# A decode kernel of two layers: late values a column at a time, the MLP's rows in two banks, and eight places for W2 blocks in place of ten

## The chip, the cores and the metric

One core of one Trainium2 chip runs the program. The metric is the device time of one execution in microseconds; the median of the runs counts. A profile of one execution, taken by the hardware profiler, shows the instructions of TensorE (PE for matmuls, PEld for weight loads), VectorE (DVE), ScalarE (ACT), GpSimd (POOL) and SyncE (SP, which here only asks for loads), the clock granted to TensorE, and the traffic of the core's 16 DMA engines.

## What is computed

One token passes twice through attention with a key and value cache and through an MLP with relu. All of it is float32; the cache of 32 heads with 8192 keys and values each is 268 MB, and both layers read the same cache and the same weights.

```python
def _A_ref(x, k_cache, v_cache, wq, wo):
    B, Sq, D = x.shape                       # 1, 1, 640
    H, Dh = 32, 128
    q = (x @ wq).reshape(B, Sq, H, Dh).transpose(0, 2, 1, 3)
    scores = jnp.einsum("bhqd,bhkd->bhqk", q, k_cache) * (Dh ** -0.5)
    p = _softmax(scores, axis=-1)
    o = jnp.einsum("bhqk,bhkd->bhqd", p, v_cache)
    return o.transpose(0, 2, 1, 3).reshape(B, Sq, H * Dh) @ wo

x = A_x
x = x + _A_ref(_layernorm(x), A_k_cache, A_v_cache, A_wq, A_wo)
x = x + relu(_layernorm(x) @ B_w1) @ B_w2
x = x + _A_ref(_layernorm(x), A_k_cache, A_v_cache, A_wq, A_wo)
x = x + relu(_layernorm(x) @ B_w1) @ B_w2
```

## The kernel before

**Loads and the ring.** Keys, values and most of W2 (12 of its 14 blocks of 128 rows) stream through one tile in SBUF, `ring`, of 4760 units; a unit is 8 float32 columns of 128 partitions, 4 KB. `todo` lists every load in order: heads 0 to 31, W2 in four runs of 4, 4, 2 and 2 blocks, then heads 31 to 0 for the second layer, and W2 again. A head's cache comes in pieces: a key piece is a row of 512 keys for each of four partition groups or a part of it, a value piece a block of 4 columns of 128 or a part of it. `pump` (L205 to 223) asks for the next load on the SP queue as soon as `place` finds room; `release` (L237) frees a piece once it is read and calls `pump`. The list is strictly in order: if the load at its head finds no room, all behind it wait. Eight semaphores serve SP's loads in turn, so a load also waits until the one eight before it has landed.

**Kept pieces.** The second layer goes through the heads backwards, so the pieces that were read last are not freed at the end of the first layer and are not loaded again. `KEPT` = 3960 units are kept: head 31, head 30 from its third unit on, and 160 units of head 29's keys. The other `W2_PLACES` = 800 units (ten blocks) are W2's at the end of the first layer; its last run waits until two blocks are read. The two small units of head 30 that are not kept are loaded beside the ring, into the tiles `wct` and `mix`, as soon as these are read for the last time (`load_beside`, L225).

**A head.** PE multiplies the keys by the query into one bank, VectorE takes maxima, ScalarE the exponentials, VectorE transposes them (`pT`), and PE multiplies the values (`values`, L526): for each of four partition groups one matmul with 4 weight columns and 512 moving columns a block, so that 16 rows come out of which 4 sums are wanted. Of the result (`outs`, 128 x 512) the right rows are summed by PE against `ind` (`summed_rows`, L572) after a copy to SBUF by VectorE and ScalarE (`copied_rows`, L565).

**The tail of a layer** begins with its last head (L819). While its keys and values land, the output projection of the others is finished, and the first part of the MLP, `hidden` (L639), is computed from them: four partition groups of 448, 448, 416 and 416 columns side by side in one bank, `acc`. The last value pieces are a whole block and two halves of one. Behind them: `copied_rows`, one matmul to keep PE busy, `summed_rows` into the column `o`, `hidden` once more with `o` and `mix` (the last head's share through the output projection and W1, combined beforehand), and the last head's output projection into `pd`. VectorE copies 256 columns of `acc` to SBUF and ScalarE the others; three matmuls (L866) turn them into columns, VectorE takes the relu into `hT`, four small matmuls (L879, L887) do the rest columns, and 14 times four matmuls (L454) multiply W2's blocks: 0, 1, 2, 3, the two rest blocks, and 4 to 11. The layer norm's spread (`deviations`, `spread_of_rows`) is computed between W2's blocks, from `pd`, and the result is scaled at the end. In the first layer the next one's layer norm and queries follow; in the last the output goes out.

## Time and profile before

| | us |
|---|---|
| median of 3 runs | 1349.75 (1349.57 to 1350.23) |
| profiled execution, its own time | 1351.18 |
| its span, first to last instruction | 1349.4 |
| PE busy in it | 800.5 (59%) |
| VectorE busy | 250.8 (19%) |
| DMA traffic | 574.52 MB, mean 426 GB/s |

The span is what the trace covers; the execution's own time has some 1.8 us more. Times in the rows are microseconds from the span's start. A DMA share of 1.00 means that all 16 DMA engines are busy; a packet counts in the stretch in which it starts, so the share can pass 1. The time to landing of a load runs from its request to the moment at which all of it is there.

### The profile page before, as it was taken

The numbers are of one execution on the slowest core, as the hardware profiler recorded it, in microseconds if no ns is written. First come the engines' busy times: TensorE is split into PE (matmuls) and PEld (weight loads), VectorE is DVE, ScalarE is ACT, GpSimd is POOL, SyncE is SP. The second block draws the span as 40 slices with busy tenths as digits, with TensorE's granted clock in tenths as the row PEclk, the third lists the DMA queues.
The fourth block names the chain that finished last, engine by engine and source line by source line (L and its number), as shares of the span: only waits on it lengthen the run. The fifth ranks groups of instructions, "written<-read, shape, count | busy, mean of one in ns | idle before, by whom it ended". The sixth has DMA issues, their size and how long they took to land.

```text
span 1349.4 us, 13603 instructions
## 1 busy us (share of the span) xinstructions
PE 800.5 (59%) x6086; PEld 271.4 (20%) x6086; DVE 250.8 (19%) x794; ACT 58.5 (4%) x149; POOL 2.9 (0%) x10
## 2 busy tenths in 40 slices
PE   3455554564755755467588765455466554756777
PEld 1111111121211211122143211112121111211223
DVE  1111121221212111122122211122111121112121
ACT  0000000000000000000000000000000000000000
POOL 0000000000000000000000000000000000000000
PEclk8787677887878787788799767788778788878789
DMA  9999999999999999999999999999999999999997
GB/s 405 436 427 430 439 439 417 446 417 445 429 432 425 444 424 429 443 413 419 427 386 427 433 439 424 431 437 422 438 435 427 423 436 434 432 415 444 419 429 314
DMA packets 22673, 574.52 MB, mean 426 GB/s; under 512 B 2516, under 2 KB 2648, under 8 KB 5464
## 3 DMA queue, kind: packets, MB, share of 16 engines
q1 hardware_dynamic: 19592, 529.84, 91.5%
q10 hardware_dynamic: 3024, 43.83, 7.6%
q8 instruction: 47, 0.77, 0.2%
q14 instruction: 10, 0.08, 0.0%
HBM read 573.65 MB, written 0.00 MB: 425 GB/s over the span
## 4 chain that ended last, share of the span: by engine, by line
DMA 64%; PE 27%; DVE 5%; ACT 1%; issue 1%; another core or an unknown queue 1%; ACTq 0%; SPq 0%; DVEq 0%
DMA ring<-in_kv 64%; PE ps L483 13%; PE outs L532 8%; DVE h_t L494 2%; DVE pt L512 1%; ACT p L508 1%; DVE p L551 1%; PE pm L499 1%; PE px L422 1%; PE acc L454 0%; PE px L454 0%; PE px L629 0%; DVE pT L514 0%; PE pm L561 0%
## 5 line engine op out<-in xcount | busy, mean ns | idle before, releaser
L483 PE MATMUL ps<-ring,spread_q 128*32 128x512 f32 (+3 forms) x2104 | 325.6, 769 | 314.7 <-DMA ring<-in_kv 309.6
L532 PE MATMUL outs<-ring,pT 128*4 128x512 f32 (+1 forms) x2080 | 267.3, 656 | 38.6 <-DMA ring<-in_kv 21.6
L483 PEld LDWEIGHTS ps<-ring,spread_q 128*32 128x32 f32 x2104 | 77.0, 137 | 498.5 <-issue 292.2
L494 DVE TENSOR_REDUCE h_t<-ps 128x1 f32<-128x512 f32 x64 | 44.3, 692 | 614.9 <-PE ps L483 614.9
L508 ACT ACTIVATE p<-ps,h_t 128x512 f32<-128x512 f32 x64 | 44.0, 687 | 1225.5 <-DVE h_t L506 1225.5
L532 PEld LDWEIGHTS outs<-ring,pT 128*4 128x4 f32 x2080 | 52.2, 92 | 194.3 <-issue 167.7
L561 PE MATMUL pm<-ones,p 128*128 128x1 f32 x120 | 23.0, 260 | 94.9 <-DVE p L551 94.9
L547 DVE TENSOR_SCALAR p<-outs,ind 128x128 f32<-128x128 f32 x60 | 21.1, 351 | 256.1 <-PE outs L532 256.1
L551 DVE SCALAR_TENSOR_TENSOR p<-outs,ind,p 128x128 f32<-128x128 f32 x180 | 63.1, 351 | 6.4
L512 DVE STREAM_TRANSPOSE pt<-p 128x512 f32<-128x512 f32 x64 | 46.5, 727 | 58.5 <-ACT p L508 58.5
L499 PE MATMUL pm<-row_of,h_t 128*128 128x16 f32 x128 | 25.7, 276 | 49.9 <-DVE h_t L494 49.0
L561 PEld LDWEIGHTS pm<-ones,p 128*128 128x128 f32 x120 | 17.8, 188 | 151.4 <-DVE p L551 150.1
L499 PEld LDWEIGHTS pm<-row_of,h_t 128*128 128x128 f32 x128 | 19.4, 191 | 110.4 <-DVE h_t L494 108.5
L422 PE MATMUL px<-pair,ln_xc 128*32 128x256 f32 x280 | 34.6, 396 | 4.4 <-ACT mix L637 4.4
L629 PE MATMUL px<-w_t,wct 128*128 128x448 f32 (+1 forms) x80 | 35.1, 553 | 1.1 <-ACT wct L622 1.1
L521 PE MATMUL pm<-ind,h_t 128*128 128x1 f32 x128 | 23.6, 254 | 18.3 <-ACT p L508 18.3
L521 PEld LDWEIGHTS pm<-ind,h_t 128*128 128x128 f32 x128 | 22.2, 202 | 37.2 <-ACT p L508 28.4
L454 PE MATMUL acc<-pair,o_cols 128*32 128x160 f32 x496 | 22.5, 323 | 0.6 <-DVE o_cols L583 0.6
L422 PEld LDWEIGHTS px<-pair,ln_xc 128*32 128x32 f32 x280 | 15.7, 113 | 21.4 <-ACT mix L637 8.5
L562 DVE TENSOR_SCALAR o_cols<-pm,h_t 128x1 f32<-128x1 f32 x60 | 13.1, 219 | 30.3 <-PE pm L561 30.3
L506 DVE TENSOR_REDUCE h_t<-pm 128x1 f32<-128x16 f32 x64 | 11.2, 175 | 32.4 <-PE pm L499 32.4
L454 PEld LDWEIGHTS acc<-pair,o_cols 128*32 128x32 f32 x496 | 15.7, 117 | 4.9 <-issue 2.4
(110 smaller groups left out, 208.4 us busy)
## 6 DMA issues: line engine op xcount, KB each, us to landing
ring<-in_kv SPq DMA_DIRECT2D x24, 4096.0 KB, 32.1
ring<-in_kv SPq DMA_DIRECT2D x11, 6144.0 KB, 35.5
ring<-in_kv SPq DMA_DIRECT2D x31, 2048.0 KB, 30.7
pair<-in_wqo ACTq DMA_DIRECT2D x13, 2560.0 KB, 24.4
ring<-in_kv SPq DMA_DIRECT2D x14, 1024.0 KB, 12.5
ring<-in_w SPq DMA_DIRECT2D x4, 1280.0 KB, 26.7
w_t<-in_w ACTq DMA_DIRECT2D x1, 4320.0 KB, 28.7
pair<-in_wqo ACTq DMA_DIRECT2D x3, 1280.0 KB, 13.0
```

Of the source, the lines that this page charges most:

```text
L422: nc.tensor.matmul(pq[32 * j : 32 * j + 32, :n], xc[:, c : c + 1].to_broadcast([P, 32]), wq_t[g][:, c, j * n : (j + 1) * n], start=(c == 0 ...
L454: nc.tensor.matmul(acc[32 * g : 32 * g + 32, :DR], col.to_broadcast([col.shape[0], 32]), wt[:, g * DR : (g + 1) * DR], start=first, stop=last,
L483: nc.tensor.matmul(hd.ps[32 * g : 32 * g + 32, c : c + n], spread_q[:, 3 - r : 35 - r], tile_of[:, at + g * n : at + (g + 1) * n], start=f ...
L494: nc.vector.tensor_reduce(hd.nm, hd.ps, AX.X, ALU.max, negate=True)
L499: nc.tensor.matmul(pt[:, :16], hd.nm.to_broadcast([P, P]), row_of.rearrange("p g r -> p (g r)"), start=True, stop=True,)
L508: nc.scalar.activation(hd.p, hd.ps, AF.Exp, bias=hd.low, scale=1.0, accum_out=hd.l)
L512: nc.vector.transpose(pt, hd.p)
L521: nc.tensor.matmul(pt[:, :1], hd.l.to_broadcast([P, P]), ind[:, 4:5], start=True, stop=True)
L532: nc.tensor.matmul(hd.out[32 * g : 32 * g + 4, r : r + m].rearrange("p r d -> p (r d)"), hd.pT[:, 4 * i : 4 * i + 4], tile_of[:, v : v + m ...
L551: nc.vector.scalar_tensor_tensor(oc[:, r], hd.out[:, r], ind[:, r : r + 1], oc[:, r - 1], op0=ALU.mult, op1=ALU.add,)
L561: nc.tensor.matmul(pt[:, :1], oc[:, 3], ones, start=True, stop=True)
L629: nc.tensor.matmul(pt[:, :n], wct[:, c], w1_t[:, c, f : f + n], start=(c == 0), stop=(c == NB - 1),)
```

## The change

- Head 29's units are cut anew: three units of keys that are loaded twice, one of 320 units that is kept, and then the four value blocks. 4120 units are kept, and W2 has 640 places (eight blocks) at the end of the first layer.
- In the tail only the first two value blocks are computed as before. The later pieces go through `late_values`: a column of `pT` at a time, spread over 32 weight columns, against 128 moving columns, summed in a bank of their own into one row a group. The row sums of the first two blocks (`sums_of_rows`) are computed behind the first late piece; at the end one copy of 128 columns and one matmul add the late sum.
- `hidden` writes columns 0 to 255 of a group into the bank `acc` and the others into `px`, so that the copy of the first bank need not wait for the second.
- The four small matmuls of the rest columns (`hidden_rest`) and the last head's output projection (`pd`) move between W2's blocks, the former ahead of the third, the latter ahead of the first rest block; the two matmuls that kept PE busy go.
- The loads into `wct` and `mix` are asked for behind W2's fourth block (`MIX_BEHIND`).

```diff
+    ("k", [(0, 0, 512), (1, 0, 128)]),
+    ("k", [(1, 128, 384), (2, 0, 256)]),
+    ("k", [(2, 256, 128)]),
+    ("k", [(2, 384, 128), (3, 0, 512)]),
+] + [("v", [v]) for v in V_ALL]
...
-DROPPED = {29: 9, 30: 2}
-KEPT = 3960
-W2_PLACES = 800
+KEPT_UNITS = {29: [3], 30: [2, 3, 4], 31: range(6)}
+KEPT = 4120
+W2_PLACES = 640
+MIX_BEHIND = 3
...
+    def late_values(hd, late, piece, where, first, last):
+
+        b, r, m = piece
+        tile_of, at = at_of[key(*where)]
+        for k in range(m):
+            for g in range(4):
+                i = 4 * (4 * b + g) + r + k
+                v = at + (g * m + k) * DH
+                nc.tensor.matmul(
+                    late[32 * g : 32 * g + 32],
+                    hd.pT[:, i : i + 1].to_broadcast([P, 32]),
+                    tile_of[:, v : v + DH],
+                    start=first and k == 0,
+                    stop=last and k == m - 1,
+                    skip_group_check=True,
+                )
+        release(*where)
...
     def hidden(ph, col, wt, first, last):
-        for g in range(4):
-            f, n = F_AT[g], F_ROWS[g]
...
+        for half, tile_of in enumerate(ph):
+            for g in range(4):
+                a = H_CUT * half
+                n = F_ROWS[g] - H_CUT if half else H_CUT
...
-        for a, (piece, at) in enumerate(pieces):
-            values(hd, piece, at, a == 0, a == len(pieces) - 1)
-            if a == 1:
+        for a, (piece, at) in enumerate(pieces[:2]):
+            values(hd, piece, at, a == 0, a == 1)
+            if a == 0:
                 next(rest)
-            if a == 2:
-                at_once(rest)
         rows = copied_rows(hd)
-        keep_busy(1, 128)
+        at_once(rest)
+        for a, (piece, at) in enumerate(pieces[2:]):
+            late_values(hd, late, piece, at, a == 0, a == len(pieces) - 3)
+            if a == 0:
+                pt = ps_m.tile([P, 512], F32, name="pm")
+                sums_of_rows(pt, rows, False)
+        o_late = work.tile([P, 2 * DH], F32, name="q_row")[:, :DH]
+        nc.vector.tensor_copy(o_late, late)
+        nc.tensor.matmul(
+            pt[:, :WIDE], o_late, one_of_each.to_broadcast([P, WIDE]), start=False, stop=True
+        )
         o = work.tile([P, 1], F32, name="c_ol")
-        summed_rows(hd, rows, o)
+        nc.vector.tensor_scalar(o, pt[:, :1], hd.rl, 0.0, op0=ALU.mult, op1=ALU.add)
...
-        nc.vector.tensor_copy(hr[:, : 2 * P], ph[:, : 2 * P])
-        nc.scalar.copy(hr[:, 2 * P : F_ROWS[2]], ph[:, 2 * P : F_ROWS[2]])
-        nc.scalar.copy(hr[:64, F_ROWS[2] :], ph[:64, F_ROWS[2] : F_ROWS[0]])
+        for c in range(2):
+            nc.vector.tensor_copy(hr[:, c * P : (c + 1) * P], ph[0][:, c * P : (c + 1) * P])
+        nc.scalar.copy(hr[:, H_CUT : F_ROWS[2]], ph[1][:, : F_ROWS[2] - H_CUT])
+        nc.scalar.copy(hr[:64, F_ROWS[2] :], ph[1][:64, F_ROWS[2] - H_CUT : F_ROWS[0] - H_CUT])
...
             if a == 2:
+                hidden_rest()
+            if a == 4:
+                times_rows(pd, wo_t[last // HG][:, last % HG], o, True, True)
...
+            if a == 7:
                 ss = deviations(x1, s1)
-            if a == 8:
+            if a == 10:
                 r1 = spread_of_rows(ss)
...
-            if L == 0 and a == 1:
+            if L == 0 and a == MIX_BEHIND:
+                load_beside(wct.rearrange("p c d -> p (c d)"), 0, NB * P)
                 load_beside(mix, 0, DFF)
```

PE in the first layer's tail, from the last head's first value block to the second `hidden`. Before (`outs` are the values' sums, `pm` the row sums, `acc<-w_t` and `acc<-mix` the two parts of `hidden`):

```order
L532 MATMUL outs_107<-ring,pT 4x512 x8
L642 MATMUL acc<-w_t,ln_xc 32x448 x2
L642 MATMUL acc<-w_t,ln_xc 32x416 x2
L532 MATMUL outs_107<-ring,pT 4x512 x4
...
L532 MATMUL outs_107<-ring,pT 4x256 x8
L388 MATMUL px<-w_t 128x128
L576 MATMUL pm<-ind,p 128x64 x4
L642 MATMUL acc<-mix,c_ol 32x448 x2
```

After:

```order
L528 MATMUL outs_107<-ring,pT 4x512 x4
L661 MATMUL acc<-w_t,ln_xc 32x256 x4
L661 MATMUL px<-w_t,ln_xc 32x192 x2
...
L546 MATMUL outs_106<-ring,pT 32x128 x16
L588 MATMUL pm<-ind,p 128x64 x4
L546 MATMUL outs_106<-ring,pT 32x128 x16
L871 MATMUL pm<-sel,q_row 128x64
L661 MATMUL acc<-mix,c_ol 32x256 x4
```

The four row sums moved from behind the last value piece to a place ahead of the last two, and behind these one matmul is left.

PE from there through W2 (`px<-ring` and `px<-w_t` with `hT` are W2's blocks, four matmuls each; `sel,wct` the turning into columns). Before:

```order
L454 MATMUL pm<-pair,c_ol 32x160 x4
L388 MATMUL px<-w_t 128x128
L866 MATMUL pt<-sel,wct 128x64
L866 MATMUL ps<-sel,wct 128x64 x2
L879 MATMUL ps<-sel,wct 64x1 x2
L887 MATMUL ps<-sel,wct 32x1 x2
L454 MATMUL px<-ring,hT 32x160 x8
L368 MATMUL pm<-x_s,sel 128x1
```

After:

```order
L892 MATMUL pt<-sel,wct 128x64
L892 MATMUL ps<-sel,wct 128x64 x2
L450 MATMUL px<-ring,hT 32x160 x8
L909 MATMUL ps<-sel,wct 64x1 x2
L917 MATMUL ps<-sel,wct 32x1 x2
L450 MATMUL px<-ring,hT 32x160 x8
L450 MATMUL pm<-pair,c_ol 32x160 x4
L450 MATMUL px<-w_t,hT 32x160 x8
```

W2's first two blocks now stand directly behind the three turning matmuls, and the rest pieces and the projection behind W2's second and fourth block.

The SP queue between the layers (W2's runs are `ring<-in_w`; the numbers are partitions x float32 columns). Before:

```order
L219 DMA ring<-in_w 128x2560 x2
L219 DMA ring<-in_w 128x1280
L229 DMA wct<-in_kv 128x640
L219 DMA ring<-in_w 128x1280
L229 DMA mix<-in_kv 128x1728
L219 DMA ring<-in_kv 128x2048 x2
```

After:

```order
L215 DMA ring<-in_w 128x2560 x2
L215 DMA ring<-in_w 128x1280 x2
L225 DMA wct<-in_kv 128x640
L225 DMA mix<-in_kv 128x1728
L215 DMA ring<-in_kv 128x2560 x2
```

W2's third run, before the last load that needed no used block, now stands with the fourth behind the reading of W2's first blocks, and `wct` and `mix` behind both.

## Rows read from the trace of the kernel before

**Rows 1.** The page, part 4: the chain that ended last, by engine.

```profile
DMA 64%; PE 27%; DVE 5%; ACT 1%; issue 1%; another core or an unknown queue 1%; ACTq 0%; SPq 0%; DVEq 0%
```

**Rows 2.** Stretch within layer 1: stretch, length, engines' busy time (instructions), PEclk, DMA, GB/s.

```profile
100.00:600.00 500.00, 279.58 (x1996) 90.57 (x1996) 88.89 (x268) 21.04 (x54) 0.00 (x0) 0.79 1.00 432
```

**Rows 3.** The same view, between the layers, 2 us each.

```profile
694.00:696.00 2.00, 2.00 (x23) 1.24 (x23) 0.49 (x2) 0.37 (x2) 0.00 (x0) 1.00 0.60 253
696.00:698.00 2.00, 1.88 (x38) 1.42 (x40) 1.00 (x8) 0.00 (x0) 0.00 (x0) 1.00 0.50 191
698.00:700.00 2.00, 2.00 (x50) 1.22 (x42) 0.68 (x4) 0.00 (x0) 0.00 (x0) 1.00 0.94 319
```

**Rows 4.** Timeline of the SP queue there: start, duration, what is asked for.

```profile
676.52 0.33 SPq L219 DMA_DIRECT2D ring<-in_w  x1
...
696.99 0.33 SPq L229 DMA_DIRECT2D wct<-in_kv  x1
697.55 0.33 SPq L219 DMA_DIRECT2D ring<-in_w  x1
```

**Rows 5.** DMA issues at 676.52 and 697.55: KB, us to landing.

```profile
ring<-in_w SPq DMA_DIRECT2D x1, 640.0 KB, 22.5
ring<-in_w SPq DMA_DIRECT2D x1, 640.0 KB, 4.3
```

**Rows 6.** Timeline, layer 1's tail: start, duration, instruction, [idle before <-releaser].

```profile
686.70 1.90 PE L532 MATMUL outs<-ring,pT 128*4 128x512 f32 x16 [0.22 <-DVE pT L514]
...
690.69 1.29 PE L532 MATMUL outs<-ring,pT 128*4 128x256 f32 x16
...
691.36 0.11 PEld L532 LDWEIGHTS outs<-ring,pT 128*4 128x4 f32 x8 [0.49 <-DMA ring<-in_kv]
...
692.05 0.42 DVE L568 COPY p<-outs 128x256 f32<-128x256 f32 x1 [5.32 <-PE outs L532]
...
692.52 1.12 PE L576 MATMUL pm<-ind,p 128*128 128x64 f32 x8
...
693.95 0.94 PE L642 MATMUL acc<-mix,c_ol 128*32 128x448 f32 x8 [0.31 <-DVE c_ol L583]
...
695.44 0.29 ACT L862 COPY wct<-acc 128x160 f32<-128x160 f32 x1 [2.51 <-DVE wct L861]
...
695.46 0.43 PE L866 MATMUL pt<-sel,wct 128*128 128x64 f32 x2
...
696.46 0.28 PE L879 MATMUL ps<-sel,wct 64*64 64x1 f32 x4
...
696.70 0.33 PE L454 MATMUL px<-ring,hT 128*32 128x160 f32 x2
```

**Rows 7.** Timeline of PE in the last tail.

```profile
1330.54 1.90 PE L532 MATMUL outs<-ring,pT 128*4 128x512 f32 x16 [0.86 <-DMA ring<-in_kv]
...
1335.47 0.61 PE L532 MATMUL outs<-ring,pT 128*4 128x256 f32 x8 [0.26 <-DMA ring<-in_kv]
...
1338.07 0.94 PE L642 MATMUL acc<-mix,c_ol 128*32 128x448 f32 x8 [0.31 <-DVE c_ol L583]
...
1340.81 0.33 PE L454 MATMUL px<-ring,hT 128*32 128x160 f32 x2
...
1344.23 1.84 PE L454 MATMUL px<-ring,hT 128*32 128x160 f32 x48
```

**Rows 8.** SP's last request for W2, and DMA issues there: KB, us to landing.

```profile
1324.62 0.33 SPq L219 DMA_DIRECT2D ring<-in_w  x1
...
ring<-in_w SPq DMA_DIRECT2D x1, 640.0 KB, 20.0
```

**Rows 9.** Two timeline rows of one shape, and the stretch of the first.

```profile
651.76 1.29 PE L483 MATMUL ps<-ring,spread_q 128*32 128x320 f32 x8 [5.90 <-DMA ring<-in_kv]
...
723.42 0.74 PE L483 MATMUL ps<-ring,spread_q 128*32 128x320 f32 x8 [1.80 <-DVE spread_q L473]
...
652.00:654.00 2.00, 1.19 (x9) 0.13 (x1) 0.69 (x1) 0.00 (x0) 0.00 (x0) 0.50 1.04 438
```

More of the change, by code (lines that the diff above doesn't have):

```diff
@@ L94 @@
 F_TILES = 3
+H_CUT = 2 * P
 F_REST = 2
@@ L118, in decode_kernel @@
     order = [(h, i) for h in range(H) for i in range(len(UNITS[h]))]
-    kept = [u for u in order if u[0] >= min(DROPPED) and u[1] >= DROPPED.get(u[0], 0)]
+    kept = [u for u in order if u[1] in KEPT_UNITS.get(u[0], [])]
     assert sum(size(UNITS[h][i]) for h, i in kept) == KEPT
-    apart = {(29, 9): (3800, KEPT), (30, 0): (4464, 4544), (30, 1): (4544, RING), (30, 2): (3072, 3800)}
+    apart = {(29, 3): (3800, KEPT), (30, 0): (RING - 296, RING - 216), (30, 1): (RING - 216, RING), (30, 2): (3072, 3800)}
     beside = [(1, u) for u in order[::-1] if u[0] == 30 and u not in kept]
@@ L570, in copied_rows, with sums_of_rows @@
         return rows
-    def summed_rows(hd, rows, col):
-        pt = ps_m.tile([P, 512], F32, name="pm")
+    def sums_of_rows(pt, rows, last):
         for r in range(4):
@@ L580, in summed_rows @@
                 start=(r == 0),
-                stop=(r == 3),
+                stop=last and r == 3,
             )
+    def summed_rows(hd, rows, col):
+        pt = ps_m.tile([P, 512], F32, name="pm")
+        sums_of_rows(pt, rows, True)
         nc.vector.tensor_scalar(col, pt[:, :1], hd.rl, 0.0, op0=ALU.mult, op1=ALU.add)
@@ L639, in hidden @@
     def hidden(ph, col, wt, first, last):
-        for g in range(4):
-            f, n = F_AT[g], F_ROWS[g]
-            nc.tensor.matmul(
-                ph[32 * g : 32 * g + 32, :n],
-                col.to_broadcast([P, 32]),
-                wt[:, f : f + n],
-                start=first,
-                stop=last,
-                skip_group_check=True,
-            )
+        for half, tile_of in enumerate(ph):
[3 more added lines that the diff above has]
+                nc.tensor.matmul(
+                    tile_of[32 * g : 32 * g + 32, :n],
+                    col.to_broadcast([P, 32]),
+                    wt[:, F_AT[g] + a : F_AT[g] + a + n],
+                    start=first,
+                    stop=last,
+                    skip_group_check=True,
+                )
     def attention_and_mlp(L, xr, s):
@@ L712, in before_last @@
             yield "pe"
-            ph = ps_m.tile([P, 512], F32, name="acc")
+            ph = [ps_m.tile([P, 512], F32, name=name) for name in ("acc", "px")]
             mlp_in.extend([xp, ph])
@@ L876, in attention_and_mlp, with hidden_rest @@
             )
-        pj = bank_tile()
-        for g in range(2):
-            nc.tensor.matmul(
-                pj[nf * g : nf * g + nf, 0:1],
-                hr[:64, tail_at : tail_at + nf],
-                sel[:64, g : g + 1],
-                start=True,
-                stop=True,
-            )
-        for g in range(2):
-            nc.tensor.matmul(
-                pj[half * g : half * g + half, 1:2],
-                hr[:, tail_at : tail_at + half],
-                sel[:, 2 + g : 3 + g],
-                start=True,
-                stop=True,
-            )
-        if L == 0:
-            load_beside(wct.rearrange("p c d -> p (c d)"), 0, NB * P)
+        pd = ps_m.tile([P, 512], F32, name="pm")
+        def hidden_rest():
+            nb = 4 * F_TILES
+            pj = bank_tile()
+            for g in range(2):
+                nc.tensor.matmul(
+                    pj[nf * g : nf * g + nf, 0:1],
+                    hr[:64, tail_at : tail_at + nf],
+                    sel[:64, g : g + 1],
+                    start=True,
+                    stop=True,
+                )
+            for g in range(2):
+                nc.tensor.matmul(
+                    pj[half * g : half * g + half, 1:2],
+                    hr[:, tail_at : tail_at + half],
+                    sel[:, 2 + g : 3 + g],
+                    start=True,
+                    stop=True,
+                )
+            nc.vector.tensor_scalar(
+                hT[:, nb : nb + 1], pj[:, 0:1], 0.0, 0.0, op0=ALU.max, op1=ALU.add
+            )
+            nc.vector.tensor_scalar(
+                hT[: 2 * half, nb + 1 : nb + 2],
+                pj[: 2 * half, 1:2],
+                0.0,
+                0.0,
+                op0=ALU.max,
+                op1=ALU.add,
+            )
         nb = 4 * F_TILES
-        nc.vector.tensor_scalar(
-            hT[:, nb : nb + 1], pj[:, 0:1], 0.0, 0.0, op0=ALU.max, op1=ALU.add
-        )
-        nc.vector.tensor_scalar(
-            hT[: 2 * half, nb + 1 : nb + 2], pj[: 2 * half, 1:2], 0.0, 0.0, op0=ALU.max, op1=ALU.add
-        )
-        x1 = work.tile([P, DR], F32, name="xr", bufs=2)
-        s1 = work.tile([P, 1], F32, name="x_s", bufs=2)
-        nc.vector.scalar_tensor_tensor(
-            x1, pd[:, :DR], 1.0, xp, op0=ALU.mult, op1=ALU.add, accum_out=s1
-        )
         po = ps_m.tile([P, 512], F32, name="px")
```

23 lines of the change are left out of this document (9 added, 14 removed).

## The prediction

> **What bounds the kernel now.** I read the chain that ended last first: two thirds of it are waits for loads into the ring [rows 1]. Then the stretches: from 100 to 600 us the 16 DMA engines are busy all the time at 432 GB/s [rows 2]; only around the end of the first layer does the share fall [rows 3]. So the kernel is a queue of loads with two soft places, the pause between the layers and the work after the last load.
>
> The pause. The DMA share is 0.60 and 0.50 from 694 to 698 us and nearly full again from 698 [rows 3]. The SP queue had asked for the third W2 run (two blocks) at 676.52; its next request, into `wct`, goes out only at 696.99, and the first request that waits for a used W2 block at 697.55 [rows 4]. A half-busy share is not an idle queue: the W2 run asked for at 676.52 took 22.5 us and so landed at 699.0, and the run asked for at 697.55 landed after 4.3, at 701.85 [rows 5]. Between the two landings lie 320 + 640 KB, 2.3 us at 432 GB/s, and 2.8 us pass. So the DMA engines that lag behind (a load has landed when its last part is there) pause for half a microsecond at most, while those ahead are idle for some 3 to 4 us.
>
> The end. The last value piece is taken at 1335.47; the MLP's hidden sum starts at 1338.07, W2 at 1340.81, and W2 ends at 1344.23 + 1.84 = 1346.07 [rows 7]. The last W2 run, asked for at 1324.62, landed 20.0 us later, at 1344.6 [rows 8]; its two blocks are the last third of the final 1.84 us and start at about 1345.46. So there are 0.8 us between loads and PE: a shorter tail can win 0.8 us at the end and no more, unless the loads come earlier as well.
>
> **Part 1: the keys kept.** 160 units of 4 KB are 640 KB that the second layer no longer loads: 1.52 us at 432 GB/s. But the places come from W2: its third run (640 KB) now waits for used blocks, so these 1.52 us move from before the pause to after it. What lies after the pause is as long as before; what decides is when the queue is fed again. Bounds: if the lagging DMA engines never pause, the whole 1.52 us are won; if the engines that idle anyway set the end, only the time by which the first request comes earlier.
>
> **Part 2: when the queue is fed again.** First the chain in the first layer, on PE. From 686.70 PE does two value pieces of a whole block, two of `hidden`, and a third block, and is through at 690.69 [rows 6]; order and columns of this work stay the same, and I count the late block, 128 columns at a time, at the same price. Then before did the two small pieces: they ended after the last landing, which PE waited for at 691.36 [rows 6]. After, the four row sums come first. They took 1.12 us [rows 6], of which I count 1.0 as PE's own. So: 690.69 + 1.0 + two small pieces of 0.43 (half of a block; two blocks in a row took 1.90 with 0.2 for the last to drain [rows 6]) + 0.2 for the last to drain = 692.75. The wait for the last landing is gone: PE arrives late, not the data. Then a copy of 128 columns instead of 256: between 0.21 and the 0.42 of the whole [rows 6], I take 0.3; one matmul like the first one of L866, 0.43 [rows 6], in place of 1.12; the multiplication as before (0.27 with its handover). With handovers of 0.06, `hidden` starts at 693.9. Before it started at 693.95 [rows 6]. **The late values win nothing at this place**: what the sums leave behind the last piece they put ahead of it, and PE has no idle time there to hide them. If it had (the pieces later, or the sums cheaper), the gain would be the 1.0; if a column at a time is dearer, by a tenth a piece, it is a loss of 0.3.
>
> Then `hidden` to W2: before 693.95 to 696.70, 2.75 us [rows 6]. The copy that opened the chain waited for the whole `hidden` (0.94) and took 0.42 [rows 6]. After, the first bank is complete after 256 of 448 columns, about 0.6; two copies of 0.3 follow, so that the first L866 starts at 1.05 instead of 1.51; ScalarE reads the other bank at 1.0 and is done at 1.5 (0.29 and a short one) [rows 6]; the L866 group (three transposes, 0.9 from first to last with handovers) is through at about 1.9, and W2 starts, since the small rest pieces (0.3) now come behind its first two blocks and the projection and the busy matmul are gone from between. So W2 starts at 695.8, 0.9 earlier. Its first two blocks took until the request at 697.55, 0.85 [rows 4, 6]: the request now goes out at 696.65. That is 0.35 before the request into `wct` (the first to feed the queue before) and 0.9 before the first W2 request.
>
> So the loads win 0.35 us by the engines that idle anyway. By the lagging ones: without the third run they are through 1.52 earlier, at 697.5 by landing; a request at 696.65, with 1.4 for the way and 1.5 for the data, lands at 699.55 instead of 699.0; of the 1.52 about 1.0 is left. **I take 0.6**, nearer the first, as 694 to 698 shows most engines idle.
>
> `wct` and `mix` are now asked for behind both W2 runs; their readers come 20 us later, so this is free. The ring holds 640 units for loads until layer 1 frees kept keys, but W2's two runs come on top of it: together the same bytes as before, 5.1 MB or 12 us, plus the 1.25 MB of queries. No second pause: W2's end moves from 702.6 to about 702.
>
> **Part 3: the end.** The same chain, from the last value piece: PE starts on the first block at 1330.5, and 3.9 + 1.0 + 0.86 + 0.2 later, at 1336.5, is through [rows 7]; `hidden` at 1337.65 instead of 1338.07, W2 at 1339.55 instead of 1340.81. Between the first W2 block and its end there were 5.26 us [rows 7]; the rest pieces (0.3) and the projection (0.35) now lie within: 5.9. End at 1345.5 instead of 1346.07: **0.55 us**. The cover is thin: block 10 would start at 1344.85, and its run landed at 1344.6. Bounds: 0.8 (loads) and −0.1 (if the late pieces are 0.1 dearer each and the first copies slower).
>
> The Trainium skill, page "TensorEngine Tiling (Array Packing)", section Key Properties, speaks against the new order: changing the tiling mode drains TensorE. The change adds three such switches to each tail (sums, 128 wide, between late pieces of 32; rest pieces between W2 blocks). The trace leaves little for one: W2's first matmul, 32 wide, starts at 696.70, before the 64-wide pieces of 696.46 are through (0.28) [rows 6]. By the rule, at the 0.04 that these rows could hide at most, 0.1 us of the sum would go; without it nothing.
>
> **The sum.** 0.6 + 0.55 = 1.15 us. The profiled execution takes 1351.18, of which 1349.40 are span; it would take 1350.0. The median of the runs is 1349.75, 1.4 below it; I take the difference off the median: 1348.6.
>
> **Rivals.**
> 1. *The swap is a wash.* The request comes no earlier than 696.99, because PE's backlog ahead of the last piece is larger than I count (0.35 suffices), and the tail wins nothing. For it: no idle PE time from 686.70 to 690.69. Against: the two banks save 0.4 to 0.9 in any case. It gives 1349.7.
> 2. *The kept keys pay in full.* The lagging engines set the end in both layers: 1.52 + 0.8 = 2.3, so 1347.45. For it: the landings at 699.0 and 701.85 hardly show a pause. Against: the request at 696.65 is too late for them by 0.5, and the engines that lag in one layer need not lag in the next.
> 3. *Slower: PE's clock falls in the last tail.* The change takes out the two matmuls that kept PE busy there. The same eight instructions of 320 columns took 1.29 us at 651.76, at a granted clock of 0.50, and 0.74 at 723.42 [rows 9]; PE had mostly waited before the first. It decides if the fall comes before W2: 5.9 us times (1.29/0.74 - 1) are 4.4 us more, 1353.0 with the rest of the gain. Against: the clock is full throughout this stretch now, and PE has more to do before the last piece, not less.
>
> **How the numbers follow.** The forecast has 0.60, the wash 0.22, the full gain 0.14, the clock 0.04. Some 0.2% (2.7 us) is what a measurement of this kernel can tell from no change. The full gain reaches 2.3 and only with an unpriced addition more than 2.7: faster 0.07, within 0.2% 0.89, slower 0.04. The range takes in the wash with 0.3 of the loss bounds and the full gain: 1347.4 to 1350.0.
>
> **What would show it.** In the profile after: the DMA share between the layers, low some 1.5 us earlier and full again from about 697.6; W2's third run asked for at about 696.6; the sums on PE ahead of the small pieces with PE busy throughout; W2 at 1.9 us behind `hidden`'s start; the last W2 run landing within half a microsecond of its use. I am wrong if the sums fall into a wait (then `hidden` starts a microsecond earlier, and rival 2 is near), if the share dips a second time after 705, or if the granted clock is below full behind the last value piece.

## The result and the profile after

The changed kernel is slightly slower: 1352.49 us, the median of 22 runs (1350.4 to 1354.05), against 1350.22 of before in 22 runs beside them; the ratio is 1.0013, 95% interval 1.0008 to 1.0019. The forecast was 1348.6 and its range ended at 1350.0. The 0.13% fall into the class "within 0.2%", which had 0.89, but on the other side than forecast: that the class was right is luck. The profiled span is 1351.1 us (before 1349.4); the profiled execution of the changed kernel is 0.5 us above its median, that of before 1.0.

Stretches between the layers of the changed kernel, for [rows 3]. Columns: stretch, length, busy time (instructions) of PE, PEld, DVE, ACT and POOL, PEclk, DMA share, GB/s.

```profile
694.00:696.00 2.00, 1.90 (x30) 1.29 (x34) 0.90 (x5) 0.37 (x2) 0.00 (x0) 1.00 0.50 210
696.00:698.00 2.00, 2.00 (x60) 1.48 (x53) 0.44 (x4) 0.00 (x0) 0.00 (x0) 1.00 0.39 72
698.00:700.00 2.00, 2.00 (x45) 1.25 (x42) 0.91 (x6) 0.00 (x0) 0.00 (x0) 1.00 0.83 307
700.00:702.00 2.00, 0.50 (x6) 0.30 (x2) 0.23 (x3) 0.00 (x0) 0.55 (x1) 1.00 1.00 297
...
706.00:708.00 2.00, 2.00 (x18) 1.59 (x17) 0.56 (x4) 0.00 (x0) 0.00 (x0) 0.50 1.03 437
...
712.00:714.00 2.00, 2.00 (x20) 0.52 (x16) 0.00 (x0) 0.00 (x0) 0.00 (x0) 1.00 0.84 317
```

The first pause is deeper (0.39 at 72 GB/s; before 0.50 at 191). There is a second one: from 712 to 714 the share is 0.84 at 317 GB/s, where before had 1.03 at 435. And TensorE's granted clock is 0.50 from 706 to 708, its lower level of 1.2 GHz.

Four longer stretches show the bytes, after first, then before, same columns:

```profile
690.00:694.00 4.00, 3.27 (x72) 2.60 (x68) 0.51 (x2) 0.07 (x1) 0.00 (x0) 1.00 0.77 315
694.00:704.00 10.00, 7.24 (x142) 4.82 (x146) 2.48 (x14) 0.37 (x2) 0.55 (x1) 1.00 0.73 249
704.00:720.00 16.00, 14.04 (x158) 7.48 (x158) 3.69 (x15) 0.78 (x2) 0.55 (x1) 0.79 0.99 396
1200.00:1300.00 100.00, 66.07 (x430) 20.65 (x433) 18.81 (x59) 4.40 (x11) 0.00 (x0) 0.80 0.99 424
```

```profile
690.00:694.00 4.00, 3.56 (x42) 1.93 (x37) 0.64 (x2) 0.37 (x1) 0.00 (x0) 1.00 1.02 424
694.00:704.00 10.00, 8.81 (x161) 6.07 (x161) 2.71 (x15) 0.37 (x2) 0.55 (x1) 1.00 0.81 310
704.00:720.00 16.00, 14.44 (x153) 6.46 (x157) 4.06 (x15) 0.78 (x2) 0.55 (x1) 0.89 1.02 421
1200.00:1300.00 100.00, 63.58 (x434) 18.92 (x426) 18.54 (x57) 4.29 (x11) 0.00 (x0) 0.81 1.00 428
```

Length times the difference in GB/s: from 690 to 704 the changed kernel is (424 - 315) x 4 + (310 - 249) x 10 = 1.05 MB behind, of which 0.63 need not be loaded any more (573.89 MB in all, before 574.52). The other 0.42 MB are 1.0 us at 432 GB/s. From 704 to 720 it loses 0.40 MB more, 0.9 us. So the kept keys are given back in the first pause, with a microsecond on top, and the second pause costs nearly another. Together they are 1.9 us, near the 2.3 between the medians. Outside the pauses the two executions drift apart by as much as a microsecond either way: summed over all packets, the changed kernel is 0.2 MB (0.5 us) ahead at 690 beyond the kept keys, and from 720 to 1300 it loses 0.48 MB (1.1 us), most of it from 1200 to 1300; I have no cause for that. The last unit of keys, for which PE waits in both kernels, is taken at 1327.38 after and 1324.60 before.

PE in the changed kernel: the first layer's tail, W2 and the start of the second layer. Columns: start, duration, instruction, [idle before <- releaser].

```profile
693.94 0.64 PE L661 MATMUL acc<-mix,c_ol 128*32 128x256 f32 x8 [0.31 <-DVE c_ol L875]
...
695.80 0.75 PE L450 MATMUL px<-ring,hT 128*32 128x160 f32 x16
...
702.05 0.75 PE L450 MATMUL px<-ring,hT 128*32 128x160 f32 x16 [1.54 <-DMA ring<-in_w]
703.90 0.94 PE L450 MATMUL px<-ring,hT 128*32 128x160 f32 x16 [1.10 <-DMA ring<-in_w]
...
707.98 2.36 PE L395 MATMUL px<-pair,ln_xc 128*32 128x128 f32 x40
...
711.84 0.64 PE L479 MATMUL ps<-ring,spread_q 128*32 128x512 f32 x4 [0.46 <-DVE spread_q L469]
```

`hidden` (693.94) and W2 (695.80) start where the prediction had them, and the SP queue follows at 696.62:

```profile
696.62 1.28 SPq L215 DMA_DIRECT2D ring<-in_w  x2
```

But the run asked for then is there only at about 702.0. The last run, asked for at 697.57, is there at 703.86 (the chain has it as one piece of 6.29 us), and PE waits 1.54 and 1.10 us for them:

```profile
697.57 6.29 DMA ring<-in_w
```

So W2 ends at 704.84 (before 702.63) and the second layer's first scores start at 711.84. In before they start at 709.08, behind one wait of 0.47:

```profile
701.88 0.75 PE L454 MATMUL px<-ring,hT 128*32 128x160 f32 x16 [0.47 <-DMA ring<-in_w]
...
705.12 2.36 PE L399 MATMUL px<-pair,ln_xc 128*32 128x128 f32 x40
...
709.08 3.21 PE L483 MATMUL ps<-ring,spread_q 128*32 128x512 f32 x28 [0.46 <-DVE spread_q L473]
```

Until these first scores the ring is full of kept keys and of the loads asked for, none of which is read; the first scores free the first places. In the changed kernel SP asks for nothing from 704.89, when W2 is read, to 712.92, a microsecond behind the start of the scores:

```profile
704.89 0.33 SPq L215 DMA_DIRECT2D ring<-in_kv  x1
...
712.92 0.33 SPq L215 DMA_DIRECT2D ring<-in_kv  x1
```

That is where the second pause comes from.

### The profile page after: what moved, and what is told of

It is laid out like the page before. It is cut to its first block, busy times and chain, and to the rows that moved or that the text cites. A ratio compares the mean times of both kernels' runs of the same rounds, so it can differ in the third digit from the quotient of the medians.

```text
span 1351.1 us, 13936 instructions
## 1 busy us (share of the span) xinstructions
PE 820.0 (61%) x6258; PEld 280.2 (21%) x6258; DVE 251.7 (19%) x798; ACT 58.6 (4%) x149; POOL 2.9 (0%) x10
## 2 busy tenths in 40 slices
DMA packets 22099, 573.89 MB, mean 425 GB/s; under 512 B 2452, under 2 KB 2584, under 8 KB 4760
## 4 chain that ended last, share of the span: by engine, by line
DMA 62%; PE 29%; DVE 5%; ACT 1%; issue 1%; another core or an unknown queue 1%; SPq 0%; ACTq 0%; DVEq 0%
DMA ring<-in_kv 59%; PE ps L479 15%; PE outs L528 8%; DMA pair<-in_wqo 2%; DVE h_t L490 2%; ACT p L504 1%; DVE pt L508 1%; PE pm L495 1%; PE px L418 1%; DVE p L565 1%; PE px L450 1%; PE acc L450 0%; DMA ring<-in_w 0%; PE px L646 0%
## 5 line engine op out<-in xcount | busy, mean ns | idle before, releaser
L479 PE MATMUL ps<-ring,spread_q 128*32 128x512 f32 (+4 forms) x2104 | 335.5, 790 | 297.9 <-DMA ring<-in_kv 293.0
L528 PE MATMUL outs<-ring,pT 128*4 128x512 f32 (+1 forms) x2032 | 270.8, 677 | 35.7 <-DMA ring<-in_kv 17.9
L646 PEld LDWEIGHTS px<-w_t,wct 128*128 128x128 f32 x80 | 13.5, 193 | 8.6 <-issue 7.0
```

The costliest lines, as they stand in the source:

```text
L479: nc.tensor.matmul(hd.ps[32 * g : 32 * g + 32, c : c + n], spread_q[:, 3 - r : 35 - r], tile_of[:, at + g * n : at + (g + 1) * n], start=f ...
L528: nc.tensor.matmul(hd.out[32 * g : 32 * g + 4, r : r + m].rearrange("p r d -> p (r d)"), hd.pT[:, 4 * i : 4 * i + 4], tile_of[:, v : v + m ...
L646: nc.tensor.matmul(pt[:, :n], wct[:, c], w1_t[:, c, f : f + n], start=(c == 0), stop=(c == NB - 1),)
```

## The experiments

The kernels are grouped by what they tell apart. The bands are 95% intervals of the ratio to the kernel before on the same chip, whose median was 1349.9 to 1350.2 us. Rows and stretches come from one profiled execution of each.

### The change in two halves

`swap_alone`: the kernel before with the new cut of head 29, 4120 kept units and eight places. `tail_alone`: the changed kernel with the old cut and ten places.

```diff
...
-DROPPED = {29: 9, 30: 2}
-KEPT = 3960
-W2_PLACES = 800
+KEPT_UNITS = {29: [3], 30: [2, 3, 4], 31: range(6)}
+KEPT = 4120
+W2_PLACES = 640
```

> The kernel before with only the ring's split changed: head 29 cut anew, 4120 units kept, eight places for W2; its tail is as before. Theory A (the queue runs dry: with the third W2 run no longer asked for ahead of the pause, every DMA engine comes to rest between the layers, restarts slowly, W2's last runs land late, layer 2 starts late): 1.5 to 3.5 us slower than before, share near 0.4 or less in some 2 us before the restart, layer 2's first scores 2 us or more later. Theory B (the new tail is what costs, not the split): between 1.5 us faster and no change.

> The changed kernel with the ring's old split (head 29 as before, 3960 units kept, ten places for W2), all of the new tail kept. Theory A: 0 to 1.2 us faster than before, the lagging DMA engines never at rest between the layers, layer 2's first scores within 1 us of before. Theory B: 1 to 2.5 us slower than before, as the changed kernel was.

The swap alone is 1354.84 us, 1.0032 [1.0019, 1.0044]; the tail alone 1350.15, 1.0002 [0.9994, 1.0011]. Theory A named the right half, but both its sizes were off: the swap costs 4.3 us, more than the 3.5 allowed, and the tail gains nothing. In `swap_alone` W2's last run is asked for behind `mix` and arrives so late that PE waits 4.25 us, and the second pause is long:

```profile
706.54 1.29 PE L448 MATMUL px<-ring,hT 128*32 128x160 f32 x16 [4.25 <-DMA ring<-in_w]
...
714.94 1.93 PE L477 MATMUL ps<-ring,spread_q 128*32 128x512 f32 x8 [0.46 <-DVE spread_q L467]
```

```profile
708.00:710.00 2.00, 1.57 (x13) 1.53 (x14) 0.55 (x4) 0.00 (x0) 0.00 (x0) 0.50 0.56 138
...
712.00:714.00 2.00, 2.00 (x31) 1.44 (x23) 0.35 (x1) 0.00 (x0) 0.00 (x0) 0.50 0.35 138
```

In `tail_alone` PE waits for no W2 run, the clock stays at 1.00, the queries take 1.30 us in place of 2.36, and the first scores start at 706.80; there is no second pause:

```profile
704.11 1.30 PE L401 MATMUL px<-pair,ln_xc 128*32 128x128 f32 x40
...
706.80 1.49 PE L485 MATMUL ps<-ring,spread_q 128*32 128x512 f32 x12 [0.46 <-DVE spread_q L475]
```

So the slowdown is the swap's. The new tail wins nothing for itself, but saves about 2.6 us (1.0032 to 1.0013) when the swap is there: by the two traces it brings `mix` behind both W2 runs and the second layer forward; which of its parts saves how much was not tested.

### mix ahead of W2

`after_mix_first` and `before_mix_first` ask for `mix` right behind the second `hidden`, which reads it last; they were to feed the idle DMA engines sooner.

```diff
     hidden(ph, o, mix, False, True)
+    if L == 0:
+        load_beside(mix, 0, DFF)
...
-                load_beside(mix, 0, DFF)
```

> The changed kernel, but the load of 864 KB into mix is asked for directly behind the last reader of mix (the second hidden), ahead of W2's third run in the SP queue. Theory A: the queue is fed at about 695 instead of 696.6, no engine rests for long, 1.5 to 3 us faster than the changed kernel, so 0 to 1.5 us faster than before. Theory B: no change against the changed kernel (within 0.4 us). A third way, that W2's runs land late because the loads crowd each other: slower still, since 864 KB now go ahead of them.

> The kernel before with the same one edit: mix asked for directly behind the second hidden, at about 695 instead of 697.9. Theory A in the form that idle DMA engines count even where the lagging ones go on: 0.5 to 1.5 us faster than before. In the form that only the lagging engines count: no change (within 0.3 us), as these never rested. If loads crowd each other: slower by up to 1 us, W2's last run landing later than 701.8.

Both miss: 1.0011 [1.0002, 1.002] and 1.0013 [1.0004, 1.0022]. The queue is fed earlier, but W2's runs land behind the 864 KB of `mix` (703.5 and 705.1 in the one, 703.5 in the other), W2 ends at 706.43 and 704.25, and the first scores start at 713.34 and 711.15. That the loads crowd each other, the last way named in either expectation, is what came for `before_mix_first`, and dearer than the 1 us allowed; the changed kernel became no slower. In these two, what is loaded first decides, not how early the engines have something to do.

### The start of the second layer

`before_late_start` puts three matmuls of 512 columns ahead of the second layer's first scores in the kernel before. `after_w2_short` leaves out the matmuls of W2's last four blocks in the first layer, so that nothing waits for the late runs.

```diff
+        if L:
+            keep_busy(3)
         spread(heads[0])
```

```diff
-            times_rows(po, wt, hT[:rows, b : b + 1], ...)
+            if L or b < 8 or b >= nb:
+                times_rows(po, wt, hT[:rows, b : b + 1], ...)
```

> The kernel before, with three idle matmuls of 512 columns on PE directly ahead of the second layer's first scores (2.6 us at full clock, up to 5 at half). Theory D (the loss is a second pause: the ring is full of kept keys, and loads stop until the second layer's first scores free some, so what counts is when these come): first scores at 712 to 714 instead of 709.1, the share dips between 711 and 716, and the run is 1 to 3 us slower than before. Theory E (the late start is only a sign, the loss is made in the first pause): within 0.4 us of before, since PE has slack in the second layer.

> The changed kernel without the matmuls of W2's last four blocks in the first layer (their loads and places stay as they are, that part of the sum is left out), so that PE waits for no late W2 run and the second layer starts earlier. Theory D: first scores at about 706 to 708 instead of 711.8, no dip at 710 to 714, 1 to 2 us faster than the changed kernel, about level with before or up to 0.5 faster. Theory E: no more than 0.4 us faster than the changed kernel.

A late start makes the second pause and the loss: first scores at 714.41, 1.0012 [1.0003, 1.0021]. Not all of the lateness is the edit's: in this execution W2's last run, which stands ahead of the edit, landed 5.81 us after its request at 697.48 (in before 4.29), and PE waited 1.99 us for it.

```profile
712.00:716.00 4.00, 3.88 (x21) 1.14 (x24) 0.00 (x0) 0.00 (x0) 0.00 (x0) 1.00 0.70 270
```

`after_w2_short` has a first pause deeper than the changed kernel's (0.47 at 137 GB/s from 696 to 700, there 0.61 at 190), but starts its scores at 708.03, has no second pause and takes 1350.53, 1.0001 [0.9992, 1.001]:

```profile
708.00:712.00 4.00, 3.97 (x20) 0.99 (x24) 0.00 (x0) 0.00 (x0) 0.00 (x0) 0.54 1.01 421
712.00:716.00 4.00, 3.07 (x30) 0.85 (x26) 0.95 (x3) 0.03 (x1) 0.00 (x0) 1.00 1.02 428
```

### The clock

In `after_busy` TensorE does three matmuls of 512 columns where it waits for W2's last two runs.

```diff
+            for _ in range({10: 2, 12: 1}.get(a, 0) if L == 0 else 0):
+                nc.tensor.matmul(bank_tile(), w1_t[:, 0, :P], w1_t[:, 1, :512], ...)
             rows = 2 * half if b == nb + 1 else P
```

> The changed kernel with three matmuls of 512 columns more in the first layer, two ahead of W2's ninth block and one ahead of the eleventh, where TensorE waits for W2's last two runs. Theory (of the 5.0 us by which layer 2's first scores are later than in tail_alone, about 1.8 are the clock, which falls in these waits): W2 ends at 704.6 to 705.2 as in the changed kernel, the granted clock stays at 1.00 from 700 to 712, W2's end to the first scores takes 5.2 us in place of 7.0, first scores at 709.9 to 710.4, the second dip is smaller, and the time is 0.4 to 1.5 us below the changed kernel's, ratio to before 1.0002 to 1.0010. Rival (the clock costs nothing, only the landing counts): first scores still at 711.5 to 712, or earlier without any gain; ratio 1.0011 to 1.0016.

1350.83 us, 1.0006 [0.9998, 1.0015]. W2 ends at 704.67, as late as in the changed kernel, but the clock stays at 1.00, the queries take 1.30 us and the first scores start at 709.86, two microseconds earlier:

```profile
703.92 0.75 PE L450 MATMUL px<-ring,hT 128*32 128x160 f32 x16
...
707.17 1.30 PE L395 MATMUL px<-pair,ln_xc 128*32 128x128 f32 x40
...
709.86 2.35 PE L479 MATMUL ps<-ring,spread_q 128*32 128x512 f32 x20 [0.46 <-DVE spread_q L469]
```

The second pause shrinks to 384 and 382 GB/s in the stretches from 712 to 716 (share 0.96 and 1.04). So about 1.8 us of the late start are the clock. That this is worth half of the loss is not shown: the intervals of the two ratios overlap (1.0006 and 1.0013), and this trace is of the kernel's fastest execution (1348.97).

The start of the second layer, from PE's rows (W2's end is its last row's start plus duration), with kernels of the sections below. "Behind" is how far the two pauses set the loads back: the bytes that were moved less than in before from 690 to 720 us (length times the difference in GB/s, as above), without the 0.63 MB that eight places need not load (0.31 with nine), at 432 GB/s.

| kernel | W2 ends | first scores | between | PEclk 706 to 708 | behind, us | ratio |
|---|---|---|---|---|---|---|
| tail_alone | 701.61 | 706.80 | 5.19 | 1.00 | -0.3 | 1.0002 |
| late_alone | 702.77 | 707.96 | 5.19 | 1.00 | -0.3 | 1.0002 |
| after_w2_short | | 708.03 | | 0.50 | 0.0 | 1.0001 |
| before | 702.63 | 709.08 | 6.45 | 0.50 | 0 | 1 |
| half_dve | 702.46 | 709.32 | 6.86 | 0.50 | 3.8 | 1.0014 |
| after_busy | 704.67 | 709.86 | 5.19 | 1.00 | 0.4 | 1.0006 |
| half_fit_busy | 704.15 | 710.02 | 5.87 | 0.82 | 0.0 | 0.9993 |
| half_fit | 703.64 | 710.58 | 6.94 | 0.50 | -0.2 | 0.9999 |
| after_dve | 704.38 | 711.15 | 6.77 | 0.50 | 0.8 | 0.9998 |
| before_mix_first | 704.25 | 711.15 | 6.90 | 0.50 | 1.2 | 1.0013 |
| after | 704.84 | 711.84 | 7.00 | 0.50 | 1.9 | 1.0013 |
| after_mix_first | 706.43 | 713.34 | 6.91 | 0.50 | 1.2 | 1.0011 |
| before_late_start | 704.09 | 714.41 | 10.32 | 0.50 | 2.3 | 1.0012 |
| swap_alone | 707.83 | 714.94 | 7.11 | 0.50 | 5.2 | 1.0032 |

The start does not settle the time by itself: `half_fit` and `after_dve` start at 710.58 and 711.15 and are level with before, `half_dve` starts at 709.32 and is not. What goes with the time is how far the loads fall behind in the pauses: up to 0.8 us the ratios are 0.9993 to 1.0006, from 1.2 on 1.0011 to 1.0032. (In the four kernels whose names hold `dve` or `half`, VectorE's sums shorten the last tail by 0.6 us, 0.0004 of the ratio.) By these rows a late start costs as far as it leaves the queue without loads.

### The tail's parts

`banks_alone` is `tail_alone` with the value pieces and row sums of before. `late_alone` is before with the late columns and the sums ahead of them; the matmul that kept PE busy ahead of the sums goes with them, the rest stays.

```diff
-        for a, (piece, at) in enumerate(pieces[:2]):
-            values(hd, piece, at, a == 0, a == 1)
+        for a, (piece, at) in enumerate(pieces):
+            values(hd, piece, at, a == 0, a == len(pieces) - 1)
...
-            late_values(hd, late, piece, at, a == 0, a == len(pieces) - 3)
...
+        summed_rows(hd, rows, o)
```

> The new tail with the places and keys of before, but with the value pieces and the four row sums as in the kernel before (no late columns); the two banks, the rest pieces and the projection amid W2 and the later request for mix stay, the two busy matmuls stay out. Theory (the earlier start of the second layer comes from the two banks and from what moved amid W2, the late columns give nothing): the second hidden starts in layer 1 at 693.7 to 694.1, W2 0.9 us earlier than before, layer 2's first scores at 706.8 to 708, no second pause, time within 0.1% of before (1349.3 to 1350.7). Rival (the late columns bring the earlier start): first scores at 708.5 to 709.1 and a time as before or slower.

> The kernel before with the late value columns and the row sums ahead of them, and nothing else: one bank for hidden, rest pieces and projection ahead of W2, ten places. Theory: the late columns give nothing; in the last tail hidden starts 2.8 to 2.9 us behind the landing of the last value piece (before 2.64) and the time is 1350.0 to 1350.6, at most 0.3 us above before; layer 2's first scores at 708.5 to 709.5. Rival (the late columns bring the earlier start): first scores at 706.8 to 708.

1349.49 us, 0.9996 [0.9987, 1.0004], and 1350.17, 1.0002 [0.9993, 1.0011]. `banks_alone` has the earlier second layer (706.87) without the late columns: the banks and what moved amid W2 end W2 0.95 us earlier (701.68), and 1.26 are the clock, which stays up as PE waits for no W2 run. The 707.96 of `late_alone` lies where the rival had it, but not by the late columns: it starts `hidden` later than before (694.31), and its gain is the clock, which stayed up there behind a wait of 0.25.

`tail_dve` and `after_dve` replace the copies and the four row sums of the first two blocks by four operations of VectorE and one matmul.

```diff
-        rows = copied_rows(hd)
+        nc.vector.tensor_scalar(oc[:, 0], hd.out[:, 0], ind[:, :1], 0.0, ...)
+        for r in range(1, 4):
+            nc.vector.scalar_tensor_tensor(oc[:, r], hd.out[:, r], ind[:, r : r + 1], oc[:, r - 1], ...)
...
-                sums_of_rows(pt, rows, False)
+                nc.tensor.matmul(pt[:, :WIDE], oc[:, 3], ones.to_broadcast([P, WIDE]), ...)
```

> The new tail on the old split (3960 kept, ten W2 places), with the sums of the first two value blocks done by VectorE (four masked operations, some 1.5 us beside PE's late block) and one matmul in place of four on PE ahead of the last two pieces. If the four sums on PE are what held the late values up: hidden starts 0.6 to 0.8 us earlier behind the last value piece in both layers, and the end comes 0.5 to 0.8 us earlier than in the same kernel with four sums, so 0.4 to 0.8 us faster than before. If the late pieces themselves are the cost: no change.

> The same edit on the changed kernel (4120 kept, eight W2 places). By theory D the 0.7 us count twice, at the second pause and at the end: 1 to 1.5 us faster than the changed kernel, still 0.3 to 1 us slower than before. If only the end counts: 0.5 to 0.8 us faster than the changed kernel.

> tail_dve once more, on the same chip as half_dve, since its lead over the kernel before was small against its interval. Theory: the lead holds, 0.5 to 1.3 us below before (ratio 0.9990 to 0.9996), layer 2's first scores at 706 to 707 and no second pause. Rival (the lead was chance): ratio 0.9997 to 1.0005.

`tail_dve` takes 1349.15 us, 0.9990 [0.9981, 0.9999], and again 1348.81, 0.9991 [0.9982, 1.0000]: the fastest of the kernels here, about 1 us below before. `after_dve` takes 1350.47, 0.9998 [0.9989, 1.0007], better than either way expected: with the cheaper sums the whole swap is level with before, 2.0 us below the changed kernel, of which 0.6 are the last tail.

The last tail, from the first value block's start to the request for the output. Rows of the changed kernel:

```profile
1332.68 1.04 PE L528 MATMUL outs<-ring,pT 128*4 128x512 f32 x8 [0.21 <-DVE pT L510]
...
1337.91 1.08 PE L546 MATMUL outs<-ring,pT 128*32 128x128 f32 x32
1340.15 0.64 PE L661 MATMUL acc<-mix,c_ol 128*32 128x256 f32 x8 [0.31 <-DVE c_ol L875]
...
1342.02 0.75 PE L450 MATMUL px<-ring,hT 128*32 128x160 f32 x16
...
1346.65 1.29 PE L450 MATMUL px<-ring,hT 128*32 128x160 f32 x32
1348.51 0.65 SPq L979 DMA_DIRECT2D out<-xr  x1
```

| tail | kernel | us |
|---|---|---|
| old | swap_alone, 1334.73 to 1350.56 | 15.83 |
| old, waiting 0.26 for the last piece | before, 1330.54 to 1346.63 | 16.09 |
| late columns only | late_alone, 1329.51 to 1345.55 | 16.04 |
| banks and moved pieces only | banks_alone, 1328.42 to 1344.00 | 15.58 |
| both | after, 1332.68 to 1348.51; tail_alone, 1329.45 to 1345.28 | 15.83 |
| both, VectorE's sums | tail_dve_2, 1329.01 to 1344.26 | 15.25 |

No wait for a DMA lies in these but the one named: the tail is PE's own chain. The late columns cost 0.2, the banks and moved pieces win 0.25, and together they are the old tail's 15.83.

### Half the swap

`half_dve` is `after_dve` with nine places, 80 units more kept than before, and W2's last runs of one, one and two blocks. `half_fit` cuts head 29's loaded keys into units of 240, 240, 240 and 64 instead of 360, 360 and 64. `half_fit_busy` adds one matmul of 512 columns ahead of W2's eleventh block.

Of the edit of `half_dve`:

```diff
-KEPT = 4120
-W2_PLACES = 640
+KEPT = 4040
+W2_PLACES = 720
```

Of that of `half_fit`, against `half_dve`:

```diff
-    ("k", [(0, 0, 512), (1, 0, 208)]),
-    ("k", [(1, 208, 304), (2, 0, 416)]),
+    ("k", [(0, 0, 480)]),
+    ("k", [(0, 480, 32), (1, 0, 448)]),
+    ("k", [(1, 448, 64), (2, 0, 416)]),
```

> The changed kernel with VectorE's sums of the first two value blocks, and half of the swap: nine places for W2 blocks and 80 more units of kept keys, W2's last runs of one, one and two blocks. Theory (the price of the swap comes with the time at which W2's last run is asked for and lands, bit by bit): W2 ends between 702 and 704, layer 2's first scores between 706.4 and 711.2, about 708.5; a small second dip; time between tail_dve and after_dve, 1349.5 to 1350.1. Rival (a threshold: as long as the keys of the second layer are asked for before the queue runs dry there is no second dip, and 80 units of 4 KB, 0.76 us, are won): no stretch below 0.97 of DMA share with under 400 GB/s from 708 to 720, time 1348.2 to 1348.8.

> half_dve with head 29's keys cut into units of 240, 240, 240 and 64 in place of 360, 360 and 64, so that three requests fit into the room that W2's blocks leave. Theory (half_dve's dip came from the cut: 720 units were free, but not 360 of them in one piece a second time): three requests of 960 KB go out by 703, no stretch below 0.9 of share from 706 to 710, first scores at 709.0 to 709.6 as in half_dve (the clock falls), time 1 to 2.5 us below half_dve, ratio to before 0.9995 to 1.0006. Rival (the dip came from the late first scores alone): ratio 1.0010 to 1.0016.

> half_fit with one matmul of 512 columns ahead of W2's eleventh block in the first layer, where TensorE waits 1.1 us in half_dve. Theory (with the clock held and the keys cut to fit there is no second pause, and the 320 KB that need not be loaded are won): granted clock 1.00 from 700 to 712, first scores at 707.4 to 707.9, no second dip, time 0.4 to 0.8 us below tail_dve, ratio to before 0.9984 to 0.9989. Rival (nine places cost by the restart of the DMA engines what the kept keys save): ratio 0.9990 to 0.9998.

`half_dve`, meant to lie between, is as slow as the whole: 1351.78, 1.0014 [1.0005, 1.0023]. Its SP queue asks for nothing between the 1440 KB request at 699.55 and 712.99; 720 units were free, but not 360 of them in one piece a second time:

```profile
712.99 0.80 SPq L215 DMA_DIRECT2D ring<-in_kv  x2
```

```profile
708.00:710.00 2.00, 1.53 (x8) 0.85 (x11) 0.55 (x3) 0.00 (x0) 0.00 (x0) 0.50 0.61 128
...
712.00:714.00 2.00, 2.00 (x16) 0.47 (x12) 0.00 (x0) 0.00 (x0) 0.00 (x0) 0.55 0.38 120
```

With the cut that fits, three requests are out by 704, and the time is 1349.81, 0.9999 [0.999, 1.0008]: some 2 us are back, though PE waited 1.95 us for W2 and the first scores came later than in `half_dve` (710.58, there 709.32). With the matmul more it is 1349.05, 0.9993 [0.9984, 1.0002]; the clock fell all the same, from 706 on, and the first scores came at 710.02. Its ratio lies where the rival had it (nine places cost as much as the kept keys save), but the theory's condition, a clock that stays up, was not met. The interval doesn't tell it from `tail_dve`; that the smaller swap wins its 320 KB isn't shown.

## Why the prediction was wrong

**Part 2, the chain in the first layer.** The starts came within 0.05 us of those put down: 693.94 for `hidden`, 695.80 for W2, 696.62 for the request. Two errors of 0.25 cancel in it: the value pieces began at 686.46 instead of 686.70, and PE was through with them 6.32 us later instead of 6.05. "The late values win nothing at this place" holds; by `late_alone` they lose a little. The Trainium skill's rule on mode switches (page "TensorEngine Tiling (Array Packing)", section Key Properties) is not to be seen: W2's stretch with three more switches took 5.92 us where 5.9 were put down without them.

**"A request at 696.65, with 1.4 for the way and 1.5 for the data, lands at 699.55"** is the first step that failed: the term for the way was too small. It landed 5.4 us after the request, not 2.9. No row of the forecast shows the 1.4; [rows 5] has 4.3 us for the same 640 KB, 2.8 beyond the data. The request at 696.62 of the changed kernel, and the one at 696.54 of `after_busy`:

```profile
ring<-in_w SPq DMA_DIRECT2D x1, 640.0 KB, 5.4
...
ring<-in_w SPq DMA_DIRECT2D x1, 640.0 KB, 4.4
```

The same load took 4.0 us in `after_dve` and 4.1 in `after_w2_short`; with ten places, beside a W2 run still in flight, the one load that waits for used blocks took 4.1 in `tail_alone` and in `late_alone`. So 1.1 to 1.5 us of the error are what such a load takes here in either case. The other 1.0 to 1.4 are of this execution: by the trace's packet records fifteen of the load's sixteen parts were through at 700.1, and the last began only at 698.94, with a packet of 1.40 us where most took 0.20. To the second run, which ends W2, the prediction gave no time of its own; it landed 6.29 us after its request (5.05, 6.31 and 6.64 in the three other kernels). The Trainium skill, page "DMA: Bandwidth & Descriptors", section Latency and other measured facts, gives 0.6 us to the first byte on this path and, for an access to the memory, 0.2 us on average and 2 at high load; with 1.5 for the data an estimate by it would be 2.3 or 4.1 us. This core moved little then (72 GB/s from 696 to 698), and yet every one of these landings took longer than the 2.3.

In place of the 0.6 us won, 1.0 was lost by 704: Part 1 said that the bytes move from before the pause to behind it, but bounded the outcome by a gain on both sides. Rival 1, the wash, had no price for a pause that becomes deeper.

**"No second pause: W2's end moves from 702.6 to about 702"** is the second, and follows from the first: W2 ended at 704.84. I treated the queue from 698 on as fed by bytes alone, and did not follow what frees the next place: the second layer's first scores, which come after W2, the layer norm and the queries. [rows 3] ended at 700 and so showed no slack there. The named sign of error, a dip behind 705, is what came.

**The clock** was rival 3, in another place. It was full in the last tail; it fell between the layers, while PE waited for W2's runs. The same fall stood in the trace of before, behind its wait of 0.47 (0.50 from 706 to 708), where the late start still cost nothing, and I had not read it.

**Part 3, 0.55 us at the end,** is nothing: 15.83 us by either tail. The late third block and the two small pieces were counted as in the old form; PE's part took 6.31 us instead of 6.0. The 0.26 that it is shorter than in [rows 7] is a wait of 0.26 that the old tail had there for the last landing. And with the loads 2.8 us later the chain began 2.1 us later (1332.68 for 1330.54).

**Part 1's bytes** are true (0.63 MB fewer), but worth nothing: 1.05 MB were not moved from 690 to 704.

## What to carry to other kernels

Buffer space given to kept data is taken from the loads that bridge a pause; before trading it, follow what frees each next place, through the pause to the first reader of the next stage, and time the chain up to there. When the engine waits on that chain, look at its clock behind the wait too. Loads that must fit in one piece should be cut to the holes that their predecessors leave.

## What the runs showed of the hardware

After a pause single packets are slow, and the share hides it: in the changed kernel 1.00 of share moved 297 GB/s from 700 to 702, and 437 at 1.03 from 706 to 708, since a packet counts as busy for as long as it takes. Of the 15 packets of 5 KB that began from 697.57 to 697.94, the first behind the pause, nine took 0.67 to 1.07 us, and one at 700.06 took 1.87; most others took 0.20. From 696 to 703, 21 of 364 data packets were over 0.3 us slower than the median of their size, from 60 to 660 us 25 of 7683. Whether standing idle makes them slow is not shown: the load into `wct` also began with packets of up to 1.08 us at 701.6 (later ones 0.10), on engines that came straight from W2. And one late part of sixteen holds up a whole load: in the case above fifteen were through at 700.1, the last at 701.7, and the load counted as landed at 702.0.

TensorE's clock fell to its lower level (1.2 GHz) after waits for W2 of 0.47 us (before), 0.66 and 4.25 (`swap_alone`), 1.54 and 1.10 (after), and in every other kernel here that waited longer than 0.47; not after 0.25 (`late_alone`), without a wait (`tail_alone`, `banks_alone`) or where work filled the wait (`after_busy`); the forty matmuls of the queries then took up to 2.36 us instead of 1.30. The Trainium skill, page "TensorE: Matmul & The Clock Gate", says that the clock follows how busy the array has been recently; these runs agree but for `half_fit_busy`, where the wait was filled and the clock fell all the same. Why, I can't say.
